# A gated linear-attention block: the folded weight's last 72 rows, the keys' sum, and one weight split

## The chip, the cores and the metric

The kernel runs on one core of a Trainium2 chip. The metric is the device time of one execution in microseconds (us). A core has five engines that run their own instruction lists and meet at semaphores: PE (TensorE, matrix products; PEld is its loading of stationary operands), DVE (VectorE), ACT (ScalarE), POOL (GpSimd) and SP (SyncE, which here only issues DMA transfers). Each engine takes its instructions strictly in the order of its list: an instruction that waits holds up everything behind it on that engine.

## The reference

With x of 2048 rows and 576 columns, 32 heads of 18 columns, and a hidden width of 4608:

```
xn  = layernorm(x)
q, k, v = xn @ wqkv, per head
pq, pk  = phi(q), phi(k)          # phi(t) = (t + 1 if t > 0 else exp(t)) + 1e-6
kv  = sum over s of pk[s] v[s]^T  # 18 x 18 per head
z   = sum over s of pk[s]         # 576 numbers: the "keys' sum"
o   = (pq @ kv) / (pq . z + 1e-6)
s   = o @ wo
g   = silu(gelu(xn @ w1 + b1) @ w2 + b2)
out = x + s * g
```

Everything is float32.

## The kernel before

**Number formats.** PE multiplies plain float32 operands in two instructions for each product. An operand of type float32r takes one instruction, with fewer bits. The kernel therefore splits most operands into a high part (a cast to float32r, on ACT) and a low part (the rest, a subtraction on DVE), and adds up three products: high x high, high x low, low x high. Only few products are made in plain float32: the state kv, the spread of z, and the folded weight.

**Stages.** First come the keys and values of 16 tiles of 128 rows, tile pair by tile pair, with the state kv summed up in PSUM (`ps_kv`) and the keys' sum z per partition in `zacc` (POOL). Then follows the projection of the queries, pair by pair (rounds r = 0 to 7). After round 0's projection, `fold_wo` multiplies the block-diagonal kv (in `kvz`) with wo, so that the rest of attention is one product with a 576 x 576 matrix, the folded weight. Then comes the gated feed-forward part in 9 chunks of the hidden width, for the first and then for the second half of the rows, with seven-product (Strassen-like) schemes for w1 and w2.

**Where the change lies.** `finish_state` runs in round 0 after its second product. It does the last pair's state on PE, multiplies a 128x128 matrix of ones with `zacc` (which sums over the partitions and spreads the sum to all of them), copies that to `zb`, and masks `ps_kv` into `kvz` with three predicated copies. `fold_wo` makes the folded weight from five groups of rows: four of 126 (7 heads) and one of 72 (4 heads). The attention product wants the folded weight in five tiles of 128 rows, the fifth with the last 64 rows twice. The 126-row pieces (`kw0` to `kw4`) are therefore shifted into 128-row tiles (`kr0` to `kr3`) by DMA on SP's queue: piece i gives its first 2i rows to the end of tile i-1, and its other 126-2i rows to the start of tile i. Those transfers have 2, 124, 4, 122, 6, 120 and 8 rows of 2304 bytes. The last group is made by two products: one of 8 rows, which completes tile 3, and one of 128 rows (the 64 rows twice), which is split straight from PSUM into `kw_h[4]` and `kw_l[4]`. The tiles are split into `kw_h`, `kw_l` by `split_kw` (or `kw_hi` and `kw_lo`): tile 0 at once, tile 1 behind round 1's products, tiles 2 and 3 in round 2 after its third and fourth.

**Rounds.** `Proj.step` makes one of seven products in the order 1, 6, 7, 5, 2, 4, 3 into four PSUM banks A, B, Z, E. Steps 2 and 3 add to banks that ACT or DVE must have read before. `at_step(base + k)` runs what is planned after product k. In round 1, `pad(0)` (ACT) fills the last 64 columns of `pbuf0`, the divided queries of round 0, and `transpose_p(0, 0)` (PE, tile `ptp`) transposes them before the round's last product. `pbuf` is filled by POOL (`den_div`) from sums on DVE (`den_sum`) of products on POOL (`den_mul`) with `zb`. First reading of the folded weight is by `Attend` in round 2.

**First chunk.** Each chunk makes two `Up` blocks of seven products (order 1, 6, 7, 5, 2, 3, 4), and then the products with w2 (`pm`). The operands of w2 are split in between, as the tables say: `PW2_FIRST` for the first chunk, by operand: step. Step k runs behind the chunk's product k, counted from 0.

What fixes the order is the program text: the instructions of each engine are kept in the order in which the code issues them.

Of the kernel before, what the change touches and what calls it, by code (L numbers as in the profile page):

```python
# [8 lines left out]
F32 = mybir.dt.float32  # L9
F32R = mybir.dt.float32r  # L10
# [5 lines left out]
P = 128  # L16
S = 2048
D = 576
HD = 288
# [11 lines left out]
G = 7 * DH  # L31
GROUPS = [(g, min(G, D - g)) for g in range(0, D, G)]
# [7 lines left out]
NSP = 14  # L40
# [7 lines left out]
def linear_attention_gated_ffn(ctx, tc, x, wqkv, wo, w1, w1e, b1, w2, b2, out):  # L48
    nc = tc.nc
    SUB, MUL, ADD = ALU.subtract, ALU.mult, ALU.add  # L50
# [34 lines left out]
    def stage(cols, name):  # L85
        t = stg.tile([P, D], F32, tag="stg", name=name)
        return t[:, :cols]
# [13 lines left out]
    def as2(ap):  # L101
        return ap.rearrange("p (a b) -> p a b", a=2)
# [486 lines left out]
    def add(step, fn, *args):  # L589
        plans.setdefault(step, []).append((fn, args))  # L590
# [256 lines left out]
    def q_tiles(r):  # L847
        return [r_bufs[(2 * r + s) % 4] for s in range(2)]

    def finish_state():  # L850
        do_state(NPAIR - 1)
        zb_ps = psT.tile([P, 2, 512], F32, tag="pt", name="zb_ps")
        for h in range(2):
            nc.tensor.matmul(zb_ps[:, h, :HD], ones, zacc[:, h * HD : (h + 1) * HD], start=True, stop=True)
        nc.scalar.copy(as2(zb), zb_ps[:, :, :HD])
        ln = GROUPS[-1][1]
        nc.vector.copy_predicated(kvz[:G, : 4 * G], mask[:G, :], ps_kv[0][:G, : 4 * G])
        nc.vector.copy_predicated(kvz[:ln, 4 * G : D], mask[:ln, :ln], ps_kv[1][:ln, :ln])
        nc.vector.copy_predicated(kvz[:ln, D:], mask[:ln, 8:ln], ps_kv[1][:ln, 8:ln])
    base = NPAIR * NSP  # L860
    add(base + 1, finish_state)
    pr = Proj(Q_ORDER[0], wkq, q_tiles(0), mu2)
    for k, i in enumerate(K_UP):
        pr.step(i)
# [39 lines left out]
    def fold_wo(hooks):  # L904

        kwt = w2rp.tile([P, 4, D], F32, tag="w2raw", name="kw03")
        kr0, kw1, kw2, kw3 = (kwt[:, i] for i in range(4))
        kw4 = stage(D, "kw4")
        kw = [kr0, kw1, kw2, kw3, kw4]

        for i, n, at in [(i, G, i * G) for i in range(4)] + [(4, 8, 4 * G), (4, P, 512)]:
            rows = GROUPS[i][1]
            for h in range(2):
                hs = slice(h * HD, (h + 1) * HD)
                ps = bank(f"ps_kw{i}{n}{h}")[:n, :HD]
                nc.tensor.matmul(  # L916
                    ps, kvz[:rows, at : at + n], wo_sb[i][:rows, hs], start=True, stop=True
                )
                if n < P:
                    (nc.vector.tensor_copy if h else nc.scalar.copy)(kw[i][:n, hs], ps)  # L920
                else:
                    nc.scalar.copy(kw_h[:, 4, hs], ps)
                    nc.vector.tensor_tensor(kw_l[:, 4, hs], ps, kw_h[:, 4, hs].bitcast(F32), op=SUB)
            if 0 < i and n < P:

                k = 2 * i
                nc.sync.dma_start(krs[-1][P - k :], kw[i][:k])
                if i < 4:
                    krs.append(stage(D, f"kr{i}"))
                    nc.sync.dma_start(krs[-1][: G - k], kw[i][k:G])  # L930
            elif i == 0:
                krs.append(kr0)
            for fn in hooks.get(i, ()):
                fn()
# [212 lines left out]
    for r in range(NPAIR + 2):  # L1147
# [44 lines left out]
        if r == 0:  # L1192
            phi_exp(a, e_bufs[0]), phi_exp(b, e_bufs[1])
            fold_wo({
                0: [lambda: phi_max(a, e_bufs[0]), lambda: phi_max(b, e_bufs[1])],
                3: [lambda: phi_add(a), lambda: phi_add(b), lambda: den_mul(0, 0), lambda: den_mul(0, 1)],
            })
            split_kw(0, nc.vector)
            den_all(0, 0)
            add(base + NSP + 2, den_all, 0, 1)  # L1200
            add(base + NSP + 7, split_kw, 1, nc.vector)
        elif r < NPAIR:
            pr = Proj(Q_ORDER[r], wkq, q_tiles(r), mu2)
            for k, i in enumerate(K_UP):
                pr.step(i)
                if (r, k) == (2, 0):
                    transpose_p(0, 1)
                if (r, k) == (1, 5):
                    transpose_p(0, 0), p_hi(0, 0), p_lo(0, 0)
                at_step(base + k)  # L1210
# [455 lines left out]


    PW2 = {1: 3, 7: 4, 3: 6}
    PW2_FIRST = {1: 3, 2: 4, 7: 6, 3: 8}
    W2_SUMS_NEXT = {5: 23, 6: 27}  # L1670
    W2_SUMS_FIRST = {4: 4, 5: 6, 6: 10}
    W2_NEXT = {1: 15, 2: 17, 7: 19, 4: 21, 5: 23, 3: 25, 6: 27}
# [20 lines left out]
    for step in range(n_chunks):  # L1693
# [12 lines left out]
        if half == 0:  # L1706
            plan_w1(add, w1t[2 * step + 1], base, **P1)
            w2c = w2t[step]
            if not step:
                w2c.src[7] = w2c.B(0, 1)  # L1710
                add(base + 2, w2c.sum7)
            for i, at in (PW2 if step else PW2_FIRST).items():
                add(base + at, w2c.hi, i)
                add(base + at, w2c.lo, i)
            if step == 0:
                for i, at in W2_SUMS_FIRST.items():
                    add(at, w2t[0].load, i)
# [147 lines left out]
```

## Time and profile before

| what | value |
|---|---|
| time, median of 3 runs | 1098.72 us (1098.72 to 1098.9) |
| the profiled execution's own time | 1097.91 us |
| its span, first to last instruction | 1096.2 us |
| PE busy | 1083.7 us, 99% of the span |
| DVE, ACT, POOL busy | 819.5, 508.9, 454.4 us (75%, 46%, 41%) |
| TensorE clock granted, mean | 0.999 |

A timeline row reads: start in us, length in us, engine, line, operation, output<-input, sizes, count; in brackets the idle time of the engine ahead of it and what ended it. SPq rows are the issuing of a DMA, not its transfer. In the chain of waits a row reads start, length, engine, tile, line and count. In a table of stretches, PEclk is the granted share of the TensorE clock.

### The profile page before, as it was taken

The page shows a single profiled execution, that of the slowest core. Times are in us where ns is not written, and L with a number is a line of the kernel's source. Part 1 is how long each engine was busy: PE and PEld are TensorE (multiplying, and loading weights), DVE is VectorE, ACT ScalarE, POOL GpSimd, SP SyncE. Part 2 cuts the span into 40 slices and gives each one's busy share as a digit, 9 for nine tenths or more (in the row PEclk, how much of TensorE's full clock was granted, in tenths as well). Part 3 has the DMA queues.
Part 4 walks back from the last instruction along what each step waited for, and adds up shares of the span by engine and source line. Part 5 has one row for each costly group of instructions (what it writes and reads, how often), then busy time and mean ns, then how long its engine had stood idle before and what let it go on. Part 6 is the DMA issues. An engine that isn't in the chain of part 4 may idle for free.

```text
span 1096.2 us, 18990 instructions
## 1 busy us (share of the span) xinstructions
PE 1083.7 (99%) x6888; PEld 1006.4 (92%) x6888; DVE 819.5 (75%) x1284; ACT 508.9 (46%) x937; POOL 454.4 (41%) x421
## 2 busy tenths in 40 slices
PE   8999999999999999999999999999999999999998
PEld 8899999999898998989989989899898998988987
DVE  6787567997688988888888888667476574664876
ACT  7766555545545455454553544524234243242342
POOL 6855434655445264452544523424224143242310
PEclk9999999999999999999999999999999999999999
DMA  5999837897989799898997669867776667667342
GB/s 195 323 283 339 294 108 233 307 369 282 365 275 357 236 333 350 277 328 282 304 363 235 225 185 358 268 216 221 231 224 219 217 223 234 216 219 233 96 148 112
DMA packets 120859, 281.78 MB, mean 257 GB/s; under 512 B 12413, under 2 KB 41853, under 8 KB 118719
## 3 DMA queue, kind: packets, MB, share of 16 engines
q1 hardware_dynamic: 115295, 269.37, 70.8%
q0 software_dynamic: 4896, 10.03, 5.4%
q8 instruction: 54, 0.88, 0.3%
q10 hardware_dynamic: 576, 1.18, 0.3%
q14 instruction: 38, 0.31, 0.1%
HBM read 172.72 MB, written 103.09 MB: 252 GB/s over the span
## 4 chain that ended last, share of the span: by engine, by line
PE 92%; ACT 3%; DVE 2%; issue 1%; DMA 1%; POOL 0%; SPq 0%; DVEq 0%; POOLq 0%; ACTq 0%
PE pm L1483 35%; PE zy L1320 10%; PE e L1320 10%; PE a L1320 9%; PE ps_s L1000 5%; PE b L1320 5%; PE pl L479 5%; PE e L423 3%; PE a L423 2%; PE z L423 2%; PE pd L1605 2%; PE ps_kva L532 1%; PE b L423 1%; PE ptp L967 1%; PE ps_kw L916 1%
## 5 line engine op out<-in xcount | busy, mean ns | idle before, releaser
L1032 ACT CAST h_h<-g 128x512 fp32r<-128x512 f32 x204 | 120.2, 621 | 137.4 <-PE pm L1483 136.2
L1035 DVE TENSOR_TENSOR h_l<-g,h_h 128x512 fp32r<-128x512 f32 x204 | 164.8, 808 | 1.9 <-ACT h_h L1032 1.9
L1491 DVE TENSOR_TENSOR macc<-macc,pm 128x576 f32<-128x576 f32 x128 | 96.2, 752 | 37.2 <-PE pm L1483 36.3
L1320 PE MATMUL a<-xH,wa 128*128 128x512 f32 x288 | 100.8, 390 | 0.0
L1450 POOL TENSOR_TENSOR mid<-g 128x512 f32<-128x512 f32 x34 | 44.9, 1321 | 100.5 <-ACT g L1328 100.5
L1328 ACT ACTIVATE g<-b,b1c 128x512 f32<-128x512 f32 x36 | 24.8, 688 | 129.6 <-DVE b L1346 129.6
L1493 DVE TENSOR_TENSOR macc<-pm,macc 128x576 f32<-128x576 f32 x90 | 68.1, 757 | 22.4 <-PE pm L1483 22.0
L1320 PEld LDWEIGHTS a<-xH,wa 128*128 128x128 f32 x288 | 54.1, 188 | 10.8
L1337 ACT COPY mid<-a 128x512 f32<-128x512 f32 x36 | 21.2, 588 | 89.4 <-PE a L1320 89.4
L1444 POOL TENSOR_TENSOR g<-g 128x512 f32<-128x512 f32 x34 | 49.5, 1457 | 26.8 <-DVE h_l L1035 25.4
L1447 POOL TENSOR_TENSOR g<-g 128x512 f32<-128x512 f32 x34 | 52.3, 1538 | 13.1 <-DVE h_l L1035 11.8
L1340 DVE TENSOR_TENSOR mid<-b,mid 128x512 f32<-128x512 f32 x36 | 24.7, 685 | 42.4 <-PE b L1320 40.5
L1320 PE MATMUL a<-xL,wa 128*128 128x512 f32 x144 | 56.2, 391 | 0.0
L1576 POOL TENSOR_TENSOR fin1l<-fin1h,fin1l 128x288 f32<-128x288 f32 x8 | 6.5, 809 | 115.3 <-DMA fin1l<-s_dram 56.9
L1320 PE MATMUL e<-xSH,wb 128*128 128x512 f32 x144 | 50.7, 392 | 1.6 <-DVE b L1346 1.6
L1320 PE MATMUL b<-xSH,w 128*128 128x512 f32 x144 | 50.3, 390 | 0.0
L1320 PE MATMUL zy<-xH,w 128*128 128x512 f32 x144 | 50.2, 389 | 0.0
L1320 PE MATMUL e<-xSH,w 128*128 128x512 f32 x144 | 50.2, 389 | 0.0
L1320 PE MATMUL zy<-xSH,w 128*128 128x512 f32 x144 | 50.2, 389 | 0.0
L1441 POOL TENSOR_TENSOR g<-g 128x512 f32<-128x512 f32 x34 | 46.8, 1378 | 2.7
L1061 POOL TENSOR_TENSOR mid<-w1raw 128x256 f32<-128x256 f32 x17 | 13.9, 817 | 77.2 <-DVE w L1035 36.3
L1328 ACT ACTIVATE g<-e,b1c 128x512 f32<-128x512 f32 x36 | 24.8, 688 | 43.2 <-DVE e L1353 43.2
(944 smaller groups left out, 3676.7 us busy)
## 6 DMA issues: line engine op xcount, KB each, us to landing
op<-w SPq DMA_DIRECT2D x68, 256.0 KB
w<-op SPq DMA_DIRECT2D x68, 256.0 KB
w2raw<-w SPq DMA_DIRECT2D x10, 1152.0 KB
op<-w2o SPq DMA_DIRECT2D x19, 576.0 KB
we<-we_dram SPq DMA_DIRECT2D x34, 320.0 KB
w1raw<-w SPq DMA_DIRECT2D x18, 512.0 KB
op_a<-wa SPq DMA_DIRECT2D x16, 512.0 KB
wa<-op_a SPq DMA_DIRECT2D x16, 512.0 KB
```

The source lines that it names most:

```text
L423: nc.tensor.matmul(ps, st, mv, start=first and n == 0, stop=n == len(seq) - 1, skip_group_check=True,)
L479: nc.tensor.matmul(self.ps[n], st, self.wk(hl, k, n), start=(i == 0), stop=(i == n_all - 1))
L1000: nc.tensor.matmul(self.ps[h], st[:, k, :], w[:, k, h * HD : (h + 1) * HD], start=(i == 0), stop=(i == len(self.seq) - 1),)
L1032: nc.scalar.copy(pair[0], src)
L1035: eng.tensor_tensor(pair[1], src, pair[0].bitcast(F32), op=SUB)
L1320: nc.tensor.matmul(ps.rearrange("p (c j) -> p c j", c=4), st, mv, start=first and n == 0, stop=n == len(seq) - 1, skip_group_check=True,)
L1328: nc.scalar.activation(g, ps, AF.Gelu_apprx_tanh, bias=b1c[:, f : f + 1])
L1444: tt(src[6, pr], src[5, pr], A(0, 0), op=ADD)
L1447: tt(src[3, pr], src[6, pr], A(0, 1), op=SUB)
L1483: nc.tensor.matmul(ps[:, q, :HD], hs[p][st][:, cs], m[:, p ^ flip, :], start=(n == 0 and i not in CHAIN), stop=(n == len(seq) - 1), skip_g ...
L1491: nc.vector.tensor_tensor(dst, dst, src, op=SUB)
L1493: nc.vector.tensor_tensor(dst, src, dst, op=ADD)
```

## The change

It has three parts.

1. **The keys' sum.** `zacc` is split into two float32r parts (`zh` on ACT, `zl` on DVE), the matrix of ones is cast to float32r, and four float32r products replace the two float32 ones. The products move from right behind the state to after round 0's fifth product.
2. **The last 72 rows.** One product of 72 rows replaces those of 8 and of 128. Its result goes to `kw4`. A new tile `kr4` gets rows 8 to 71 of it twice, by two more DMAs of 64 rows on SP's queue, behind the seven others. Tile 4 is split by `split_kw(4)` in round 1 after its fourth product, and no more from PSUM. The third predicated copy falls away.
3. **First chunk.** Operand 3 of w2 is cast (`hi`) after step 5 and subtracted (`lo`) after step 6, where both were after step 8.

```
     def finish_state():
         do_state(NPAIR - 1)
-        zb_ps = psT.tile([P, 2, 512], F32, tag="pt", name="zb_ps")
-        for h in range(2):
-            nc.tensor.matmul(zb_ps[:, h, :HD], ones, zacc[:, h * HD : (h + 1) * HD], start=True, stop=True)
-        nc.scalar.copy(as2(zb), zb_ps[:, :, :HD])
...
-        nc.vector.copy_predicated(kvz[:ln, D:], mask[:ln, 8:ln], ps_kv[1][:ln, 8:ln])
+    def split_z():
+        ones_r = t1.tile([P, P], F32R, tag="x_tmp0h", name="ones_r", bufs=1)
+        z_hl = [t1.tile([P, D], F32R, tag=f"e{i}", name=f"z{v}", bufs=1) for i, v in enumerate("hl")]
+        nc.scalar.copy(ones_r, ones)
+        nc.scalar.copy(z_hl[0], zacc)
+        nc.vector.tensor_tensor(z_hl[1], zacc, z_hl[0].bitcast(F32), op=SUB)
+        cur["z"] = ones_r, z_hl
+    def spread_z():
+        ones_r, z_hl = cur.pop("z")
+        zb_ps = psT.tile([P, 2, 512], F32, tag="pt", name="zb_ps")
+        for h in range(2):
+            for i in range(2):
+                nc.tensor.matmul(
+                    zb_ps[:, h, :HD], ones_r, z_hl[i][:, h * HD : (h + 1) * HD], start=(i == 0), stop=(i == 1)
+                )
+        nc.scalar.copy(as2(zb), zb_ps[:, :, :HD])
     base = NPAIR * NSP
     add(base + 1, finish_state)
+    add(base + 2, split_z)
+    add(base + 4, spread_z)
...
-        for i, n, at in [(i, G, i * G) for i in range(4)] + [(4, 8, 4 * G), (4, P, 512)]:
-            rows = GROUPS[i][1]
+        for i, (at, n) in enumerate(GROUPS):
+            rows = n
...
-                if n < P:
-                    (nc.vector.tensor_copy if h else nc.scalar.copy)(kw[i][:n, hs], ps)
-                else:
-                    nc.scalar.copy(kw_h[:, 4, hs], ps)
-                    nc.vector.tensor_tensor(kw_l[:, 4, hs], ps, kw_h[:, 4, hs].bitcast(F32), op=SUB)
-            if 0 < i and n < P:
+                (nc.vector.tensor_copy if h else nc.scalar.copy)(kw[i][:n, hs], ps)
+            if 0 < i:
                 k = 2 * i
                 nc.sync.dma_start(krs[-1][P - k :], kw[i][:k])
-                if i < 4:
-                    krs.append(stage(D, f"kr{i}"))
-                    nc.sync.dma_start(krs[-1][: G - k], kw[i][k:G])
+                krs.append(stage(D, f"kr{i}"))
+                nc.sync.dma_start(krs[-1][: n - k], kw[i][k:n])
+                if i == 4:
+                    nc.sync.dma_start(krs[-1][n - k :], kw[i][k:n])
...
             add(base + NSP + 2, den_all, 0, 1)
+            add(base + NSP + 3, split_kw, 4, nc.vector)
             add(base + NSP + 7, split_kw, 1, nc.vector)
...
-    PW2_FIRST = {1: 3, 2: 4, 7: 6, 3: 8}
+    PW2_FIRST = {1: 3, 2: 4, 3: 6, 7: 6}
...
             for i, at in (PW2 if step else PW2_FIRST).items():
-                add(base + at, w2c.hi, i)
+                add(base + at - (i == 3 and not step), w2c.hi, i)
                 add(base + at, w2c.lo, i)
```

Three places show how the instructions move. The first is ACT's list from the end of the fold to round 1's first transposes. Before (`a` is bank A of round 1, `scr` the query tile, `pbuf` the divided queries that PE transposes next):

```order
L922 CAST kw_h<-ps_kw_2162 128x288
L922 CAST kw_h<-ps_kw_2166 128x288
L896 CAST kw_h<-kw_2114 128x576
L435 COPY scr<-a_2179 128x288
L447 ACTIVATE scr<-a_2179,c_84 128x288
L959 COPY pbuf_2109<-pbuf_2109 128x64
L974 CAST th_2243<-ptp_2237 128x640
```

And now, from the same place on:

```order
L935 COPY kw_2122<-ps_kw_2162 72x288
L912 CAST kw_h<-kw_2121 128x576
L435 COPY scr<-a_2181 128x288
L912 CAST kw_h<-kr_2169 128x576
L447 ACTIVATE scr<-a_2181,c_84 128x288
L972 COPY pbuf_2116<-pbuf_2116 128x64
L987 CAST th_2247<-ptp_2241 128x640
```

The cast of tile 4 (`kr_2169`) now stands between two readings of bank A, ahead of the copy into `pbuf` (`pad(0)`) that PE's transposes wait for.

The second place is SP's queue behind the fold, as it is now. `kr_2138`, `kr_2147`, `kr_2156` are tiles 1, 2, 3 and `kr_2169` is tile 4; the 128-row rows after them reload x:

```order
L941 DMA kr_2138<-kw_2121 124x576
L939 DMA kr_2138<-kw_2121 4x576
L941 DMA kr_2147<-kw_2121 122x576
L939 DMA kr_2147<-kw_2121 6x576
L941 DMA kr_2156<-kw_2121 120x576
L939 DMA kr_2156<-kw_2122 8x576
L941 DMA kr_2169<-kw_2122 64x576
L943 DMA kr_2169<-kw_2122 64x576
L405 DMA xL<-x_dram_99 128x768
```

The two transfers of 64 rows are new; the first seven transfers keep their shapes and their order.

The third place is DVE in the first chunk, where the second `Up` block begins (`w_0__` are operands of w2, `mid` the helper sums). Before:

```order
L1357 TENSOR_TENSOR zy_3685<-zy_3685,mid 128x512
L1035 TENSOR_TENSOR w_0__3805<-w2raw_3667,w_0__3805 128x576
L1340 TENSOR_TENSOR mid<-b_3814,mid 128x512
L1035 TENSOR_TENSOR w_0__3837<-w2raw_3667,w_0__3837 128x576
L1343 TENSOR_TENSOR mid<-zy_3815,mid 128x512
L1035 TENSOR_TENSOR h_l<-g,h_h 128x512
L1346 TENSOR_TENSOR b_3814<-e_3816,mid 128x512
```

And now:

```order
L1371 TENSOR_TENSOR zy_3689<-zy_3689,mid 128x512
L1048 TENSOR_TENSOR w_0__3795<-w2raw_3671,w_0__3795 128x576
L1048 TENSOR_TENSOR w_0__3814<-w2raw_3671,w_0__3814 128x576
L1354 TENSOR_TENSOR mid<-b_3823,mid 128x512
L1357 TENSOR_TENSOR mid<-zy_3824,mid 128x512
L1048 TENSOR_TENSOR h_l<-g,h_h 128x512
L1360 TENSOR_TENSOR b_3823<-e_3825,mid 128x512
```

Both subtractions of w2 now stand ahead of the second block's first sum, operand 3's ahead of operand 7's, and none stands between the first and the second sum.

## The prediction

> **What bounds the kernel now.** I read the page first, then the chain of waits and the timeline around the two places that the change touches.
>
> ```profile
> PE 1083.7 (99%) x6888; PEld 1006.4 (92%) x6888; DVE 819.5 (75%) x1284; ACT 508.9 (46%) x937; POOL 454.4 (41%) x421
> PE 92%; ACT 3%; DVE 2%; issue 1%; DMA 1%; POOL 0%; SPq 0%; DVEq 0%; POOLq 0%; ACTq 0%
> ```
>
> PE is busy 99% of the span and carries 92% of the chain that ended last. So PE work that goes is gained, and every microsecond that PE waits is lost. The profiled execution took 1097.91 us, 1.71 more than its span of 1096.2; the median of the runs is 1098.72, 0.81 above the profiled one. My sum is a difference to the profiled execution, and I add it to the median.
>
> **Products that go.** The chain of waits shows PE around the fold (start, length, what, count):
>
> ```profile
> 153.20 1.02 PE zb_ps L854 x4
> 154.22 0.80 PE z L423 x6
> 159.27 6.32 PE ps_kw L916 x24
> 165.59 0.79 PE a L423 x6
> ```
>
> Two float32 products are four instructions of 1.02/4 = 0.255 us; a float32r one takes 0.79/6 = 0.132. The spread of z goes from 1.02 to 4 x 0.132 = 0.53 us: 0.49 gained. The fold goes from 24 instructions to 20, and 4 x 0.255 = 1.02 go. Its 6.32 us also hold 0.2 of waits for banks (6.32 - 24 x 0.255); between none and all of that goes too, and I take 0.1. The low part of z is a DVE subtraction behind this one:
>
> ```profile
> 155.08 0.45 DVE L441 TENSOR_TENSOR scr<-z,scr 128x288 f32<-128x288 f32 x1
> 153.17 0.74 DVE L175 TENSOR_TENSOR wkq_rl<-rr,wkq_rh 128x576 fp32r<-128x576 f32 x1
> ```
>
> One predicated copy less lets the first row start about 0.1 earlier; then a subtraction like the second row's ends near 156.2. PE comes to the spread at 153.20 + 22 x 0.132 = 156.1 (three products of round 0 are ahead of it, with 6, 8 and 8 instructions): a wait of 0 to 0.2, I take 0.1. PE thus comes 0.4 earlier to the fold and 1.5 earlier to what follows. ACT's two more casts for z fall into its idle time there.
>
> **The wait that is added.** Tile 4 of the folded weight now goes over SP's queue, and ACT must cast it in the middle of round 1. The timeline, ACT first, then SP's issues, then POOL, PE and DVE:
>
> ```profile
> 166.50 0.40 ACT L435 COPY scr<-a 128x288 f32<-128x288 f32 x1
> 170.18 0.50 ACT L447 ACTIVATE scr<-a,c 128x288 f32<-128x288 f32 x1 [3.28 <-PE a L423]
> 170.58 0.23 ACT L959 COPY pbuf<-pbuf 128x64 f32<-128x64 f32 x1
> 172.46 0.68 ACT L896 CAST kw_h<-kr 128x576 fp32r<-128x576 f32 x1
> 178.66 0.68 ACT L896 CAST kw_h<-kr 128x576 fp32r<-128x576 f32 x1 [0.69 <-DMA kr<-kw]
> 179.75 0.67 ACT L896 CAST kw_h<-kr 128x576 fp32r<-128x576 f32 x1 [0.42 <-DMA kr<-kw]
> 162.59 0.74 SPq L927 DMA_DIRECT2D kw<-kw  x1
> 163.38 0.65 SPq L930 DMA_DIRECT2D kr<-kw  x1
> 164.15 0.60 SPq L927 DMA_DIRECT2D kr<-kw  x1
> 164.84 1.01 SPq L930 DMA_DIRECT2D kr<-kw  x1
> 165.95 0.88 SPq L927 DMA_DIRECT2D kr<-kw  x1
> 166.93 0.82 SPq L930 DMA_DIRECT2D kr<-kw  x1
> 167.86 0.68 SPq L927 DMA_DIRECT2D kr<-kw  x1
> 168.59 1.64 SPq L405 DMA_DIRECT2D xL<-x_dram  x1
> 168.88 1.17 POOL L950 TENSOR_TENSOR pbuf<-rt,den 128x576 f32<-128x576 f32 x1 [2.02 <-DVE den L947]
> 170.97 0.71 PE L967 MATMUL ptp<-ident,pbuf 128*128 128x128 f32 x5
> 171.18 0.46 DVE L431 SCALAR_TENSOR_TENSOR scr<-z,scr 128x288 f32<-128x288 f32 x1
> ```
>
> The three casts from `kr` are tiles 1, 2 and 3. Those of tiles 2 and 3 stand late in the order and still waited for their transfers: tile 2 (122 and 6 rows, issued at 164.84 and 165.95) was there at 178.6, tile 3 (120 and 8 rows, issued at 166.93 and 167.86) at 179.7. So tile 3 took 12 us from its last issue. That is a queue and not the size: tile 3 came 1.09 us after tile 2, issued 2 us apart.
>
> The Trainium skill gives a cause ("DMA: Bandwidth & Descriptors", section "Why a DMA increments its semaphore by 16 and not by 1"): a transfer is spread over the largest number of rings up to 16 that divides its outermost dimension, the lowest-numbered ones. By that rule 122 rows lie on two rings, 61 each, while 64 rows take all 16, these two included; the trace agrees in so far as tile 2 was 12.7 us on its way (165.95 to 178.66), and by the rule tile 4 can't pass it.
>
> Tile 4's two halves are issued at the place where `xL` stands, right behind tile 3. I take it that they land behind tile 3 as tile 3 landed behind tile 2, since both tiles have 128 rows in all: 1.1 us later. With the 0.4 by which the whole fold comes earlier, tile 4 is there for ACT at 179.75 + 1.1 - 0.4 = 180.4. The bounds: 179.3, if its own rows take nothing, and 181.5, if each half takes 1.1.
>
> The cast stands in ACT's list between the copy at 166.50 and the reading of bank A at 170.18. Behind it, in ACT's order, are that reading, `pad(0)` (the row at 170.58), and then the casts of the transposed queries. PE's transposes at 170.97 need `pad(0)`. From 180.4: the cast needs 0.6 until the next starts (0.68 less the overlap that such rows show), the reading 0.40 (170.58 - 170.18), and from `pad(0)`'s start to PE's transposes it is 170.97 - 170.58 = 0.39. So PE starts them at 181.8, where the row of before says 170.97: **10.9 us late**. The gain of 1.5 is eaten: it brings PE there at 169.5, from where it idles 12.3 us. POOL's half (168.88 + 1.17) was not last before and isn't now. DVE is held too, since its subtraction for tile 4 stands ahead of its row at 171.18; it is free near 182.4, before the first subtraction of the transposed queries can start.
>
> **A colder PE.** Rows from the end and the start of the execution (stretches: length, busy times, granted clock in the seventh place, DMA share, GB/s):
>
> ```profile
> 1090.32 0.56 PE L1619 MATMUL pd7b<-w__11930,xSL 128*128 128x288 f32 x3
> 1092.00:1094.00 2.00, 0.00 (x0) 0.00 (x0) 1.00 (x3) 0.19 (x1) 0.00 (x0) 0.88 0.22 78
> 1094.00:1096.00 2.00, 0.00 (x0) 0.00 (x0) 0.00 (x0) 0.00 (x0) 0.00 (x0) 0.50 0.22 74
> 1.67 3.85 PE L521 MATMUL warm<-ident 128*128 128x128 f32 x20 [1.67 <-POOL ident masks.py:199]
> ```
>
> PE's last product ends at 1090.9, and the granted clock falls to 0.50 within the next 3 us (0.88 over the stretch from 1092: about 1093.5). So 12 us of idle leave PE at half clock. How long it stays there at the return: the first 20 transposes took 3.85 us, where five later ones took 0.71, about 0.11 each without the last one's tail, so 2.2 for 20. The cold start cost 1.6 us. Against that, the waits that PE now has in round 1 and 2 for ACT and DVE are covered by a slower PE:
>
> ```profile
> 173.56 0.53 PEld L967 LDWEIGHTS ptp<-ident,pbuf 128*128 128x128 f32 x5 [0.25 <-issue]
> 179.20 0.19 PEld L423 LDWEIGHTS e<-wkq_h,xSH 128*128 128x128 f32 x1 [0.29 <-DVE rt L431]
> ```
>
> They are about 0.4 together. I take 1.6 - 0.4 = **1.2**; bounds 0 and 2.
>
> The Trainium skill has the same state ("TensorE: Matmul & The Clock Gate", Part 1): after an idle window of about 3.4 us the clock is halved, and about 3.4 us of work bring it back; an estimate by that page is 1.7 us lost, where the warm-up row gives 1.6.
>
> **First chunk.** DVE holds PE once here:
>
> ```profile
> 295.19 0.69 ACT L1328 ACTIVATE g<-zy,b1c 128x512 f32<-128x512 f32 x1
> 295.78 0.66 ACT L1032 CAST w__3805<-w2raw 128x576 fp32r<-128x576 f32 x1
> 296.48 1.40 DVE L1035 TENSOR_TENSOR w__3805<-w2raw,w__3805 128x576 fp32r<-128x576 f32 x1 [1.31 <-ACT w__3805 L1032]
> 298.40 1.25 DVE L1035 TENSOR_TENSOR w__3837<-w2raw,w__3837 128x576 fp32r<-128x576 f32 x1
> 300.77 0.69 DVE L1346 TENSOR_TENSOR b<-e,mid 128x512 f32<-128x512 f32 x1
> 301.51 0.50 PE L1320 MATMUL e<-xSH,wb 128*128 128x512 f32 x1 [0.96 <-DVE b L1346]
> ```
>
> DVE idles 1.31 us for ACT's cast, then does two subtractions of w2 that are both ahead of the sum at 300.77. Now operand 3's cast comes first, ahead of the activation at 295.19 that delayed operand 7's (0.59 from start to start), so DVE starts about 0.5 earlier; the rest of its work up to the sum is the same. PE's wait of about 1.1 falls by 0.5; bounds 0 (the moved subtraction is slowed by POOL as much as it gains) and 1.1 (all of it).
>
> **Sum.** The stall ends 10.9 late, cold clock 1.2, first chunk -0.5: +11.6. On the profiled execution 1109.5, on the median **1110.3 us**, 1.1% slower. Bounds: -1.1 and +1.1 for tile 4's landing, -1.2 and +0.8 for the clock, -0.6 and +0.5 for the chunk: 1107.4 to 1112.7.
>
> **Rivals.**
> - *Tile 4 is not held by the slow transfers but still queues somewhat.* Tile 1's cast at 172.46 didn't wait, so its transfers landed within 8.3 us of the issue at 164.15. If tile 4 takes 8 us from its last issue (about 168.9 with the shift of 0.4), it lands at 176.9, 3.5 earlier than I say: 1106.8. For it: its halves are smaller than any 120-row piece. Against it: tile 3's tail of 8 rows, smaller still, took 12. Chance 0.07.
> - *Not slower: tile 4 lands as it is issued.* Two issues of some 0.7 us from 168.59 - 0.4 on end near 169.7. A landing there lets PE start its transposes at 171.1, 0.1 late, and with the first chunk the sum is 0.4 faster: 1098.3. Each microsecond of landing costs one more, so it decides at 172.3, up to which the time is within 0.2% of before (2.2 us). This is also the best that the change can do, since PE's gain of 1.5 ends at this cast. For it: 64 rows are little. Against it: no `kr` transfer that ACT waited for landed so fast. Chance 0.05.
> - *A longer stall.* The x reloads or the halves' own slots hold tile 4 or its second half by 2 us more, or PE stays cold for two windows: 1112 to 1114. Against it: the reloads stand behind tile 4 in the queue. Chance 0.08.
>
> The forecast has 0.80. A difference of 0.2% (2.2 us) is about what a measurement of this kernel can tell from none. Slower by more than that: the forecast, the first and the third rival, 0.95, less 0.03 for a mistake of mine in reading the order: 0.92. Within: most of the second rival and half of the mistake, 0.06. Faster: 0.02. The range takes in the bounds and most of the first rival: 1106 to 1113.
>
> **What would show it.** In the changed kernel's timeline, ACT's cast from `kr` between the copy and the reading of bank A in round 1 must show an idle of about 15 us that ends by a DMA `kr<-kw` near 180.4, and PE's first `ptp` about 12 us of idle, ending near 181.8. The granted clock in the stretch behind it must fall to 0.5 for about 3 us. The fold must have 20 instructions in about 5.2 us, the spread of z four in 0.53. PE's wait at the second `Up` block's step 3 (`e<-xSH,wb`) must fall to about 0.6. If PE's transposes start before 173, the queue argument is wrong, and with it the forecast; if they start near 181.8 and the time is not near 1110, the later part of the sum is.

## The result, and the profile after

| | time, median (us) | beside it, before | ratio, 95% interval |
|---|---|---|---|
| the change | 1109.34 (1107.01 to 1110.27, 5 runs) | 1098.72 (5 runs) | 1.0095 [1.0084, 1.0105] |

The change is 10.6 us slower. The forecast was 1110.3, with 1106 to 1113 as its range. The profiled execution took 1109.34 us, with a span of 1107.6. It is the median of its runs, while the profiled execution of before was 0.81 below its own median, so the two traces differ by 11.4 us and the medians by 10.6.

The waits of PE between 150 and 330 us name the place (tile and line, what was waited for, us in total, times, longest):

```profile
PEld ptp L980 <- ACT pbuf L972: 9.7, 1, 9.7
PEld z L423 <- DVE scr L441: 1.1, 1, 1.1
PEld pm L1497 <- ACT h_h L1045: 0.8, 1, 0.8
```

And the chain of waits through this stretch (start, length, what):

```profile
156.15 0.62 PE zb_ps L869 x4
156.76 1.06 PE z L423 x8
157.83 1.07 PE e L423 x8
158.90 5.06 PE ps_kw L932 x20
...
168.47 1.43 SPq L941
...
169.94 9.27 DMA kr<-kw
...
179.29 0.67 ACT kw_h L912
179.97 0.40 ACT scr L447
180.37 0.14 ACT pbuf L972
...
180.55 0.47 PE ptp L980
```

Where the chain of before ran through PE alone, it now leaves PE for tile 4's transfer: 9.27 us from the start of its last issue to its landing, then ACT's cast, ACT's reading of bank A, ACT's `pad(0)`, and only then PE. The timeline of ACT and PE shows the same from the waiting side:

```profile
165.03 0.40 ACT L435 COPY scr<-a 128x288 f32<-128x288 f32 x1
179.29 0.67 ACT L912 CAST kw_h<-kr 128x576 fp32r<-128x576 f32 x1 [13.87 <-DMA kr<-kw]
179.87 0.49 ACT L447 ACTIVATE scr<-a,c 128x288 f32<-128x288 f32 x1
170.49 0.60 PE L980 MATMUL ptp<-ident,pbuf 128*128 128x128 f32 x4
180.55 0.47 PE L980 MATMUL ptp<-ident,pbuf 128*128 128x128 f32 x1 [9.46 <-ACT pbuf L972]
```

One thing is new in it: four of the five transposes ran at 170.49, and only the fifth waited, since only the last columns of `pbuf` come from `pad(0)`.

How late PE is against before, read from the start of the same product in both traces (us; the last line compares the spans):

| place | before | change | difference |
|---|---|---|---|
| first product behind the spread of z | 156.98 | 156.60 | -0.4 |
| end of the fold | 164.69 | 163.07 | -1.6 |
| round 1's z (waits for DVE) | 169.92 | 169.31 | -0.6 |
| first product behind the first transposes | 171.44 | 180.68 | +9.2 |
| 8 us on | 179.44 | 190.04 | +10.6 |
| round 4 | 240.44 | 250.74 | +10.3 |
| first chunk, `e<-xSH,wb` | 301.51 | 310.71 | +9.2 |
| later chunk | 570.54 | 582.13 | +11.6 |
| span | 1096.2 | 1107.6 | +11.4 |

At 100 us, ahead of all that the change touches, PE stands level in these two traces (0.02 apart). In the traces of the runs below it does not: there it is 0.5 us ahead in the late cast, 0.4 with both edits together, 0.2 to 0.6 in the three kernels that are built on the late cast, and 1.5 late with part 3 alone. What is said below of PE being ahead or late holds that amount too.

The stretches behind the wait show the clock (length, busy times of PE, PEld, DVE, ACT, POOL, granted clock in the seventh place, DMA share, GB/s):

```profile
172.00:174.00 2.00, 0.00 (x0) 0.00 (x0) 0.00 (x0) 0.00 (x0) 0.00 (x0) 1.00 0.92 205
174.00:176.00 2.00, 0.00 (x0) 0.00 (x0) 0.00 (x0) 0.00 (x0) 0.00 (x0) 0.70 1.00 315
...
182.00:184.00 2.00, 2.00 (x10) 2.00 (x10) 1.79 (x4) 0.94 (x2) 0.00 (x0) 0.50 1.05 397
184.00:186.00 2.00, 2.00 (x14) 1.98 (x14) 1.53 (x3) 1.84 (x4) 0.01 (x1) 0.74 1.03 416
186.00:188.00 2.00, 2.00 (x17) 2.00 (x16) 1.51 (x3) 2.00 (x5) 1.88 (x2) 1.00 0.21 83
```

PE stops at about 171.1, the clock halves at about 174.8 (0.70 over the stretch from 174), and it is back at about 185.0, some 4.5 us after PE's return. The products start 0.24 us apart at half clock (181.06 to 183.94 holds twelve such steps) and 0.13 at full clock.

### The profile page after: what moved, and what is told of

It is laid out like the page before. It is cut to its first block, busy times and chain, and to the rows that moved or that the text cites. A ratio compares the mean times of both kernels' runs of the same rounds, so it can differ in the third digit from the quotient of the medians.

```text
span 1107.6 us, 18985 instructions
## 1 busy us (share of the span) xinstructions
PE 1085.7 (98%) x6884; PEld 1008.5 (91%) x6884; DVE 823.0 (74%) x1283; ACT 509.8 (46%) x938; POOL 455.2 (41%) x421
## 4 chain that ended last, share of the span: by engine, by line
PE 90%; DVE 3%; DMA 2%; ACT 2%; issue 1%; POOL 0%; SPq 0%; DVEq 0%; POOLq 0%; ACTq 0%
PE pm L1497 34%; PE zy L1334 10%; PE a L1334 9%; PE e L1334 9%; PE ps_s L1013 5%; PE b L1334 5%; PE pl L479 5%; PE e L423 3%; PE a L423 2%; PE z L423 2%; PE pd L1619 2%; PE ps_kva L532 1%; DMA op<-w 1%; PE b L423 1%; DMA kr<-kw 1%
```

## The experiments

My theory: almost the whole loss is ACT's wait for tile 4, and tile 4 is late because its rows stand behind tile 2's 122 rows, which lie on two DMA engines. The rivals: something else of the change costs too; the transfers are slow for another reason; the clock costs nothing.

The trace keeps a record of each DMA engine's end of a transfer. Here are those of the folded weight's transfers in the change (us; the count is the number of engines that reported):

```
piece             issued   engines  ends
tile 1, 124 rows  163.02      4     168.55 168.58 170.27 170.40
tile 2, 122 rows  164.48      2     175.22 177.55
tile 3, 120 rows  166.59     15     13 from 169.98 to 172.96, then 176.12 178.19
tile 4, half 1    168.29     16     14 from 172.57 to 173.42, then 176.70 179.03
tile 4, half 2    169.94     16     14 from 173.13 to 174.87, then 177.43 179.22
```

So 122 rows were carried by two engines. Of each large piece behind them on the same queue, 13 or 14 engines were done 4.9 to 6.4 us after its issue, and the last two only after the two ends of the 122 rows (175.22 and 177.55). The records have no engine's number; that these two are the same engines each time is inferred from their times. That is the rule that the prediction drew from the Trainium skill ("DMA: Bandwidth & Descriptors", section "Why a DMA increments its semaphore by 16 and not by 1": the largest number up to 16 that divides the rows); the counts 4, 2, 15 and 16 agree with it. Whether this is the cause of the time is for the runs to say.

### Tile 4 cast later

The first line is in round 2's plan, the second in round 1's.

```
+            add(base + NSP + 4, split_kw, 4, nc.gpsimd)
...
-            add(base + NSP + 3, split_kw, 4, nc.vector)
```

> The change, with the cast and the subtraction of folded weight's tile 4 taken out of round 1 and put into round 2, among the steps in which tiles 1 to 3 are treated (its low part on POOL). Its two 64-row transfers stay as they are, right behind those of tile 3. My theory (PE's 9.5 us of idle is ACT's wait for these transfers, handed on through the copy that PE's transposes need): the cast finds its data, PE's idle ahead of its first transposes (ptp) falls under 1 us, PE comes to them about 1.1 to 1.5 us earlier than in the kernel before, and the granted clock stays at 1.0. Time 1096.5 to 1098.5 us, so 10.8 to 12.8 less than the change. Rival (the transfers disturb PE's way whatever waits for them, say by the x reloads that stand behind them): PE is still late at its scores or their clock stretch, and the time stays above 1105.

Measured: 1097.83 us beside 1098.73 of before, ratio 0.9994 [0.9985, 1.0003]: 11.5 less than the change. The granted clock is 0.999 in the mean, and PE no more waits for `pbuf` ahead of its first transposes. The transfer itself is as slow as ever; the chain of waits shows tile 2's last rows, waited for in round 2:

```profile
165.10 12.02 DMA kr<-kw
```

What follows: the loss is the wait, not the traffic. The transfers' time alone costs little as long as nobody on PE's way asks for them early. But the fold's full gain did not come out either: PE was 2.1 us ahead of before at the end of the fold and 1.0 ahead behind round 1's z (0.5 of both was there at 100 us). The reason stands in DVE's timeline, beside POOL's and the row of before:

```profile
164.69 1.95 DVE L915 TENSOR_TENSOR kw_l<-kw,kw_h 128x576 fp32r<-128x576 f32 x1 [0.71 <-ACT kw_h L912]
168.33 0.46 DVE L441 TENSOR_TENSOR scr<-z,scr 128x288 f32<-128x288 f32 x1
164.60 1.43 POOL L950 TENSOR_TENSOR scr<-rt,zb 128x576 f32<-128x576 f32 x1
```
```profile
166.63 0.83 DVE L899 TENSOR_TENSOR kw_l<-kw,kw_h 128x576 fp32r<-128x576 f32 x1
165.42 1.43 POOL L937 TENSOR_TENSOR scr<-rt,zb 128x576 f32<-128x576 f32 x1
```

Before, DVE had two subtractions from PSUM to do first and came to tile 0's when POOL was at the end of its product: 0.83 us. Without them, and with the shorter fold, it comes 1.9 us earlier and POOL's product only 0.8, so that they run side by side: 1.95 us, and the end of the row is 0.61 behind POOL's end. Before, it ended 0.61 behind POOL's end too (167.46 and 166.85). The sum at 168.33 stands behind it, and PE's z waited 1.1 us for that. The change's own trace has the same row with 1.96 us, hidden there by the long wait that follows.

The Trainium skill ("SBUF — State Buffer", section "Who interferes with whom") says that DVE and GpSimd share one pair of SBUF ports as an exclusive lock, held for a whole instruction, while the loser waits. The rows agree: DVE ends 0.61 us behind POOL, a little less than the 0.76 that such a subtraction takes where POOL idles (with both edits together, below, at 166.69).

### Tile 4 on another queue

```
-                nc.sync.dma_start(krs[-1][: n - k], kw[i][k:n])
+                q = nc.scalar if i == 4 else nc.sync
+                q.dma_start(krs[-1][: n - k], kw[i][k:n])
...
-                    nc.sync.dma_start(krs[-1][n - k :], kw[i][k:n])
+                    q.dma_start(krs[-1][n - k :], kw[i][k:n])
```

> The change, with the two 64-row transfers of tile 4 issued by ACT rather than by SP; the same 16 DMA engines move them. Two theories of why tile 4 landed only at 179.2. A: it stands behind the bytes of tiles 2 and 3 on the same queue, so another queue lets it past: it lands 2 to 3 us after its issue, by about 172, ACT's cast no longer waits for 13.9 us, PE's idle falls under 2 us, and the time is 1097 to 1099.5 us (ACT pays about 1 us for the two issues, which lies in its idle time). B: the DMA engines themselves are busy with tiles 2 and 3, or such a transfer takes 9 us by itself: it lands at 177 or later, and the time stays at 1107 to 1110 us.

Measured: 1102.3 us beside 1098.73, ratio 1.0035 [1.0024, 1.0047]. Neither theory's number: 7.0 less than the change, 3.6 more than before. The chain of waits:

```profile
164.33 0.53 ACTq L942
...
164.89 8.09 DMA kr<-kw
...
174.32 0.33 PE ptp L981
```

Tile 4 is issued 5 us earlier and lands 6 us earlier, but it still takes 8.09 us. Of its first half 14 of 16 engines are done by 169.20 and the other two at 169.92 and 171.19; the last ends of all are 172.06 and 172.99. Another queue lets tile 4 past the rows that wait on SP's queue, but two engines are still late with it, as would be so if they serve both queues in turn. The Trainium skill has this too ("DMA: Bandwidth & Descriptors", section "Queues, rings and completion order": an engine takes turns between its queues).

### Rows that spread

```
-                nc.sync.dma_start(krs[-1][: n - k], kw[i][k:n])
+                m = 112 if i in (1, 2) else n - k
+                nc.sync.dma_start(krs[-1][:m], kw[i][k : k + m])
+                if m < n - k:
+                    nc.sync.dma_start(krs[-1][m : n - k], kw[i][k + m : n])
```

> The change, with tile 1's 124-row piece sent as 112 and 12 rows, and tile 2's 122-row piece as 112 and 10 rows; SP's queue and the order are the same, with two issues more (about 1.4 us on SP). Theory A: a transfer's rows lie on few DMA engines where its number of rows has a small divisor (122 = 2 x 61: in the profile before only two engines carry it, for 12 us), and whatever comes behind on these engines waits; with 112 = 16 x 7 rows all engines share it. Then tiles 2, 3 and 4 land within 3 to 4 us of their issue, tile 4 by 172 to 174, PE's idle falls to 1 to 4.5 us, and the time is 1098.5 to 1102 us. Theory B: the delay is of the queue (order of issue, a fixed time for each transfer): tile 4 lands at 179 to 181 and the time stays at 1108 to 1111 us.

Measured: 1103.43 us beside 1098.73, ratio 1.0043 [1.0031, 1.0055]: 5.9 less than the change, and 1.4 above what theory A gave. The list of DMA issues (tile, queue, count, KB each, median us to landing) and the chain:

```profile
kr<-kw SPq DMA_DIRECT2D x2, 252.0 KB, 2.8
kr<-kw SPq DMA_DIRECT2D x2, 144.0 KB, 3.8
```
```profile
169.76 3.62 DMA kr<-kw
...
173.46 0.67 ACT kw_h L912
```

With the same bytes, the same queue and the same order, tile 4 takes 3.62 us where it took 9.27, and the 112-row pieces 2.8. The number of rows in a piece is the cause of the slow transfer. What is left is the issuing: SP issues tile 4's second half only at 169.76, behind ten others of 0.54 to 0.83 us each. PE's wait for `pad(0)` is 4.0 us in this trace, and that again costs the clock (0.50 in every stretch from 174 to 180), so that PE is 3.4 late behind the wait and 5.2 late 8 us on.

The same with tile 2's piece alone (`112 if i == 2`):

> The change, with tile 2's 122-row piece alone sent as 112 and 10 rows (tile 1's 124 rows stay one piece, its two transfers have four engines at most in common with tile 4's rows). Theory A (the 122 rows on two engines hold everything that comes behind them): tile 4 lands about 3 us after its issue, by 172 to 174, as with both pieces spread, PE's transposes start at 173.5 to 175.5, and the time is 1101 to 1104 us. Rival (the 124-row piece of tile 1 holds tile 4 as much): it lands at 175 or later, and the time is 1105 us or more.

Measured: 1102.94 us beside 1098.4, ratio 1.0041 [1.0026, 1.0057]; ACT's cast finds tile 4 at 173.80 and PE's wait is 4.4 us. The 122 rows alone hold tile 4; sending the 124 rows in two pieces as well makes no difference that these runs show.

Both edits together, spread pieces and tile 4 on ACT's queue:

> The change, with both of the edits that were tried apart: the pieces of tiles 1 and 2 sent as 112 rows and a rest, and tile 4's two transfers issued by ACT. My theory: each alone leaves one of two causes. On ACT's queue tile 4 was issued early, but landed only at 173, since its rows on two DMA engines share them with the 122-row piece; with the pieces spread it went through in 3 us, but SP issued it only at 170.3. Both together: issued by 166, landing by 168 to 169.5, so ACT's copy is not late for PE, the clock stays at 1.0, and the time is that of the late cast, 1097 to 1098.5 us. Rival (a transfer of 64 rows needs 7 us in this place for another reason, such as ACT's queue being slow to start): landing 172 or later, 1100 us or more.

Measured: 1098.12 us beside 1098.43, ratio 0.9999 [0.999, 1.0008], the time of the late cast within the runs' spread. ACT's timeline:

```profile
165.47 0.47 ACTq L947 DMA_DIRECT2D kr<-kw  x1
165.99 0.67 ACT L912 CAST kw_h<-kw 128x576 fp32r<-128x576 f32 x1 [1.87 <-DMA kr<-kw]
166.56 0.39 ACT L435 COPY scr<-a 128x288 f32<-128x288 f32 x1
168.84 0.67 ACT L912 CAST kw_h<-kr 128x576 fp32r<-128x576 f32 x1 [1.88 <-DMA kr<-kw]
```

Tile 4 lands at 168.8 and ACT waits 1.88 us for it, which does not make PE late: its transposes start at 170.82, where before had 170.97. But the fold's gain is gone by then. ACT's cast for tile 0 (165.99) stands behind its two issues, 1.87 us idle; DVE's subtraction for tile 0 and the sum behind it come later with it, and PE waits for that sum:

```profile
169.64 0.40 PE L423 MATMUL z<-wkq_h,xH 128*128 128x288 f32 x1 [1.30 <-DVE scr L441]
```

With tile 4 on ACT's queue alone it is the same (1.32 us at this place). The two causes, two engines for 122 rows and SP's place in the order, are thus separate, and taking away one of them alone leaves 3.6 to 4.7 us of loss.

### The change without the fold

The kernel before with parts 1 and 3 of the change only.

> The kernel before with two of the three parts: the spread of the keys' sum by float32r parts, and the split of w2's operand 3 moved in the first chunk; the fold of the last rows and the way of tile 4 are as before. My theory (the whole loss is tile 4's wait): no idle of PE ahead of its transposes beyond that of the kernel before; PE gains 0.4 us at the spread and 0.5 to 1.2 us in the first chunk, of which later waits may take some back. Time 1097.4 to 1098.5 us, ratio to the kernel before 0.9988 to 0.9998. Rival (a part of the loss comes from the other two parts, say the later small waits seen in the second half of the change's trace): 1099 us or more.

Measured: 1097.56 us beside 1098.73, ratio 0.9992 [0.9984, 1.0001]. So parts 1 and 3 cost nothing that these runs show; whether they gain is at the edge of what they tell. PE is 0.45 ahead from the spread of z up to round 4, as part 1 was costed. In the first chunk it gains 1.1 more at the sum of 301.51, and loses 1.2 at 314 us, behind DVE, which waits for the load of a bias:

```profile
313.07 0.75 DVE L1514 TENSOR_TENSOR macc<-mid,pm 128x576 f32<-128x576 f32 x1 [1.56 <-DMA mid<-b]
```

### Part 3 alone

```
-    PW2_FIRST = {1: 3, 2: 4, 7: 6, 3: 8}
+    PW2_FIRST = {1: 3, 2: 4, 3: 6, 7: 6}
...
-                add(base + at, w2c.hi, i)
+                add(base + at - (i == 3 and not step), w2c.hi, i)
```

> The kernel before with the third part alone: w2's operand 3 cast and subtracted one step earlier in the first chunk. What the prediction says: PE's wait of 1.1 us at the second Up block's step 3 falls by about 0.5 and the rest of the time follows: 1098.2 us, ratio 0.9995. Rival (as the kernel with two parts showed: the wait goes, but PE waits about 1.3 us later on, for the halves of h): 1098.5 to 1099.2 us, no difference that can be measured.

Measured: 1098.55 us beside 1098.43, ratio 1.0003 [0.9994, 1.0011]: no difference. The wait that it aims at did fall, by 0.4 us (PE's waits between 150 and 330 us, before and with part 3 alone):

```profile
PEld e L1320 <- DVE b L1346: 1.4, 1, 1.4
```
```profile
PEld e L1320 <- DVE b L1346: 1.0, 1, 1.0
```

It is 0.9 to 1.0 too in the late cast, the other queue, the spread pieces and the warm PE below, and 0.6 in both edits together. It vanished in the change, in the change without the fold, and in the fastest kernel below. In the change this has a reason: DVE's row `b<-e,mid` stands at 309.79 there and at 309.39 in the run with the warm PE below, 0.4 apart, while PE is ready for it at 310.71 in the one and at 309.4 in the other, 1.3 apart. DVE is ahead of PE in the one and 0.7 behind it in the other. So this wait took up 0.7 us of what the cold clock had cost. Why it vanished in the other two is not shown.

### PE kept warm

```
+        if (r, s) == (0, 0):
+            for _ in range(84):
+                nc.tensor.transpose(pt[:, KT * P : (KT + 1) * P], ident, ident)
```

> The change, with 84 transposes of the identity more on PE, into columns of the transposes' tile that nobody reads, just ahead of the transposes that wait for tile 4 (about 9 us of PE work in the place of its idle time). The wait itself stays. My theory (of the loss, 1.0 to 1.3 us is PE's halved clock after the idle time): the granted clock stays at 1.0 from 172 to 188, the products after the wait take 0.13 us each at once, and the time is 1107.7 to 1108.6 us, 0.8 to 1.5 below the change. Rival (the clock costs next to nothing, since PE would wait for ACT and DVE there anyway): within 0.4 of the change, 1109.0 to 1109.8 us.

Measured: 1107.12 us beside 1098.43, ratio 1.0079 [1.0065, 1.0093]: 1.9 nearer to before than the change is (8.7 against 10.6), though the two intervals overlap, and 0.6 below the range that I gave. The stretches:

```profile
172.00:176.00 4.00, 4.00 (x39) 4.00 (x38) 0.00 (x0) 0.00 (x0) 0.00 (x0) 1.00 0.99 255
176.00:180.00 4.00, 4.00 (x39) 3.91 (x36) 0.00 (x0) 0.57 (x1) 0.00 (x0) 1.00 0.56 157
180.00:184.00 4.00, 3.41 (x26) 3.06 (x25) 3.23 (x6) 2.68 (x7) 0.00 (x0) 1.00 1.03 406
```

The clock stays at 1.00. PE is 9.3 late behind the wait and 9.0 late in round 4, where the change is 9.2 and 10.3 late. Between these two places the cold clock therefore cost 1.1 against before, and 1.4 against a PE that stays warm and has the small waits of before. At the first chunk's sum 0.6 of this is left.

### A version that beats both

First the late cast with tile 0's subtraction on POOL, so that DVE's sum is not held by it (`split_kw(0, nc.gpsimd)` for `split_kw(0, nc.vector)`):

> The kernel of the late cast (the change, with tile 4 cast in round 2), with the subtraction for the folded weight's tile 0 on POOL rather than on DVE. There this subtraction took 1.95 us on DVE beside POOL's product, where before it took 0.83 behind POOL's, and PE waited 1.1 us for DVE's sum at 168.8 that stands behind it. My theory (the shorter fold has moved DVE's subtraction onto POOL's time, and the wait takes back what the fold gains): with the subtraction on POOL, behind its product, DVE comes to the sum by 167.5, the 1.1 us of PE's wait are gone, PE reaches its transposes 2.0 us earlier than in the kernel before, and the time is 1096.3 to 1097.4 us, about 1 less than the late cast. Rival (POOL's own next work, which the transposes need, comes later by the 1.4 us and PE waits there): 1097.5 to 1098.5 us.

Measured: 1097.81 us beside 1098.43, ratio 0.9994 [0.9985, 1.0003], the rival's number, but not for its reason. The wait at z is gone, and PE is 1.9 ahead at the first transposes. It loses 1.3 at the second ones:

```profile
177.63 0.67 ACT L912 CAST kw_h<-kr 128x576 fp32r<-128x576 f32 x1 [1.59 <-DMA kr<-kw]
180.13 1.44 POOL L915 TENSOR_TENSOR kw_l<-kr,kw_h 128x576 fp32r<-128x576 f32 x1 [2.58 <-ACT kw_h L912]
182.16 1.17 POOL L963 TENSOR_TENSOR pbuf<-scr,den 128x576 f32<-128x576 f32 x1 [0.59 <-PE ps_s L1013]
183.38 0.77 PE L980 MATMUL ptp<-ident,pbuf 128*128 128x128 f32 x5 [1.05 <-POOL pbuf L963]
```

The casts of tiles 2 and 3 wait for their slow transfers, tile 4's cast and subtraction follow them, and POOL's row for the second transposes follows these. So the pieces of tiles 1 and 2 were spread as well:

> The kernel with tile 4's late cast and tile 0's subtraction on POOL, and besides with the pieces of tiles 1 and 2 sent as 112 rows and a rest. In the former kernel PE was 1.9 us ahead of the kernel before at its first transposes and lost 1.2 of it at its second ones (183.4), where it waited for POOL's row, which stood behind tile 4's subtraction, which waited for the casts of tiles 2 and 3, which waited 1.6 us for their transfers. My theory: with the pieces spread these casts find their data, POOL's subtraction starts about 1.5 us earlier, and the wait at 183.4 is gone: PE is 1.8 to 2.1 us ahead at 240, and after what later waits take back the time is 1096.2 to 1097.3 us, ratio 0.998 to 0.999. Rival (the order of the casts, not the transfers, sets POOL's time there, or the later waits give back whatever is gained before): 1097.5 to 1098.3 us, as the two kernels before it.

Measured: 1096.9 us beside 1098.4, ratio 0.9985 [0.9976, 0.9994]: faster than before by 0.15%, and 12 us faster than the change. PE's waits for `pbuf` and z are gone, and PE is 2.2 us ahead in round 4 and 3.3 at the first chunk's sum (0.35 of both from before 100 us). Later it gives back 2.4 of that (0.9 ahead at 570), for the most part in waits for one of DVE's sums (PE's waits from 330 us on, before and in this kernel):

```profile
PEld e L1320 <- DVE b L1346: 1.8, 3, 0.9
```
```profile
PEld e L1337 <- DVE b L1363: 3.7, 6, 0.9
```

The same with part 3 taken back:

> The same kernel with the third part of the change (w2's operand 3 a step earlier in the first chunk) taken back. The prediction says that this part is worth 0.5 us: the time is then 0.3 to 0.6 above that of the kernel with it. Rival (as the kernel with the third part alone showed, 1098.55 beside 1098.43): no difference within 0.3.

Measured: 1096.94 us beside 1098.4, ratio 0.9985 [0.9977, 0.9994]. Part 3 has no worth here either that these runs show. In the traces PE gains 1.1 with it at the first chunk's sum, where it loses 0.2 without it, and both kernels end within 0.2 us of each other.

Not tried: part 1 alone, and tile 4 sent ahead of tile 2 in SP's order.

## Why the prediction was right, and where it was off

The place, the mechanism and the sign were as forecast. Its steps:

- **Products that go.** The spread takes 0.62 us in the chain with a small wait for `zl` in it (forecast 0.53 and a wait of 0.1), and PE is 0.4 ahead behind it. The fold takes 5.06 (5.2), and PE is 1.6 ahead (1.5). What the step left out is DVE's order: without two subtractions from PSUM, DVE's subtraction for tile 0 meets POOL's product and takes 1.96 us for 0.83, and 1.0 of the 1.6 was gone at round 1's z. In the change the later wait hides that. In the late cast, without that wait, it takes most of what the fold is worth.
- **Tile 4's landing.** Forecast 180.4, measured 179.22, at the lower bound (179.3). The prediction added 1.1 to tile 3's landing and took off 0.4 for the earlier fold. Against tile 3's own end (178.37) the 1.1 measured 0.85. The other part is that tile 3 itself ended 1.3 earlier than the 179.67 of before, not 0.4. Why is not shown; the x reloads are issued later in the change.
- **What PE does at the landing.** Forecast: transposes start 10.9 late at 181.8. Measured: the fifth at 180.55, and the next product 9.2 late. Of the 1.7 between, 1.1 is the landing, and some 0.4 is that four of the five transposes need nothing of `pad(0)` and ran before. I took the whole tile for one; the row of before said x5 and hid it. By the letter of my sign ("if PE's transposes start before 173") the four at 170.49 would speak against the forecast; the sign holds for the one that waited, and I should have named it.
- **A colder PE.** Forecast 1.2 (bounds 0 and 2). The products behind the wait lose 1.1 up to round 4, and the run with the warm PE confirms the size in its trace. The two parts of the term were both off and made up for each other: PE ran at half clock for 4.5 us after its return, which is some 2.2 us of work (half of 4.5) and not 1.6, and the waits that before had there took up about 1.1 of it and not 0.4. By the times of the runs alone it could be anything from 0 to 3.8 us (1.9, and about as much to each side, from the two intervals).
- **First chunk.** Forecast -0.5, and 0.4 was what the wait itself fell by in the runs without a cold PE. In the change's own trace the whole wait went (-1.1 against round 4), 0.7 of that as it took up part of the cold clock; but none of it reached the end in the runs that tested part 3.
- **The sum.** In the trace, -0.6 (z), +9.8 (the wait), +1.1 (clock and small waits), -1.1 (first chunk) make +9.2; the forecast was 11.6. Later small waits, for DVE's h_l and sums, add 2.2 that the prediction doesn't have, so the trace ends at +11.4. Not all of that is the change's: in each of the twelve other traces, the change's among them, PE loses against the trace of before behind the first chunk's sum, by 0.3 (part 3 alone) to 2.4 us. So the profiled execution of before was probably a fast one there, and part of the 2.2 is its own. By medians it is +10.6. That the forecast came so near is thus partly luck: the wait was overestimated by 1.7 and the first chunk's gain underestimated by 0.6, and the 2.2 that the later chunks give back were left out.

The rivals: tile 4 did not pass the slow transfers in the change; it had to be sent another way, in rows that spread, to do so. Then the rival for "somewhat queued" comes true in kind: 1102.94 and 1103.43, with ACT's cast of tile 4 at 173.80 and 173.46. The point from which the second rival decides was put at a landing of 172.3; with both edits it landed at 168.8, and the time was that of before. The third, a longer stall, did not come: 1109.34 is below its 1112.

## What to carry to other kernels

In these runs a transfer's price was set not by its bytes alone but by its number of rows, its place in the queue and what shared its engines: 112 rows took 2.8 us, 122 rows 13 (issued at 164.48, ended at 177.55), and the tail of everything behind them too. Before an instruction is put into the middle of an engine's list, ask when its operand lands, not when it is issued, and what stands behind it: here a cast whose result PE reads only at 183.57 in the trace of before held a copy that PE needed at 170.97 there. And when work goes from an engine, its next instruction comes earlier, into the time of another; look at whom it meets there.

## What the runs showed of the hardware that was not expected

- The clock can fall after PE is at work again. With tile 4 on ACT's queue PE idled for 2.90 us and was back at 174.32; the granted clock was 0.92 over 175 to 176 and 0.50 over 176 to 179:

```profile
174.32 0.33 PE L981 MATMUL ptp<-ident,pbuf 128*128 128x128 f32 x1 [2.90 <-ACT pbuf L973]
175.00:176.00 1.00, 1.00 (x9) 1.00 (x8) 0.59 (x1) 1.00 (x3) 0.00 (x0) 0.92 0.71 217
176.00:177.00 1.00, 1.00 (x6) 0.98 (x6) 0.96 (x4) 0.10 (x2) 0.00 (x0) 0.50 0.24 88
```

It fell at about 175.8, 1.5 us after PE's return. So a wait of some 3 us (with another of 1.32 ahead of it, at 169.65) can already cost the clock: that kernel was 3.0 late behind the wait and 3.9 late 8 us on.
- The half clock came in steps of 3.41 us. The clock records of the traces give 0.50 for 10.24 us in the change (174.79 to 185.03), 6.83 with both pieces spread (173.26 to 180.08), and 3.41 each with tile 4 on ACT's queue (175.83 to 179.24) and with tile 2's piece alone spread (174.37 to 177.79). It fell 2.3 to 3.7 us after PE had stopped in the three that were still idle then. A step more or less shows: 8 us behind the wait, both pieces spread are 5.2 late and tile 2's alone 4.3, though the latter's tile 4 came later.
- A queue of its own does not make a transfer fast: tile 4 on ACT's queue took 8.09 us, though no other piece of the folded weight stood ahead of it on that queue. The 122 rows on SP's queue ended 13.06 us after their issue there, and 13.07 in the change.
- A gain ahead of the feed-forward chunks does not last: of 3.3 us at the first chunk's sum, 0.9 were left at 570 us in the fastest kernel. PE's products there wait in part for DVE's sums, and one of those waited for the load of a bias.
